# Where the second MoE's raw weight loads stand in the load queue of a fused attention, ELU MoE and SoLU MoE

## The chip, the cores and the metric

The kernel runs on one core of a Trainium2 chip. The metric is the device time in microseconds (us). The engines are TensorE (PE in the profile), VectorE (DVE), ScalarE (ACT), GpSimd (POOL) and SyncE (SP), which here issues all transfers.

## What is computed

The reference has three stages, one behind the other:

```python
# attention, keys and values averaged over groups of 8; 8 batches, 8 heads, 576 tokens, head size 64
scores = scale * q @ k_p.T;  attn = softmax(scores);  x = attn @ v_p      # x: 4608 tokens x 512
# first MoE, 512 -> 2048 -> 512
h = x @ w_in;  g = where(h > 0, h, exp(min(h, 0)) - 1);  x = g @ w_out
# second MoE, 512 -> 1024 -> 512
h = x @ w_in2;  solu = h * softmax(h);  ln = (solu - mean) / sqrt(var + 1e-6) * g_ln;  out = ln @ w_out2
```

The weights of both MoEs come as 64-bit floats. The kernel loads them as raw 64-bit integers and makes 32-bit floats of them by shifts and masks; then it splits every 32-bit operand of a large product into a high and a low part and computes three products (high x high, high x low, low x high).

## The kernel before, in words

The 4608 tokens are cut into nine blocks of 512 (j = 0 to 8). The first MoE goes block by block, each in 16 slots (f = 0 to 15), one per 128 columns of its hidden layer: `m_h1` (line 413) makes the hidden columns h by 12 matmuls and their exponential on ACT; `m_elu` (428) finishes them with two DVE instructions and makes the high part gh on ACT; `m_glo` (437) makes the low part gl on DVE; `m_o1` (444) multiplies them with the slot's rows of w_out by 12 more matmuls, one slot later. `w_out_split` (398) makes the two parts of these rows, on ACT and POOL. When a block is done, `m_out` (457) copies its result to SBUF and stores it to a DRAM buffer x1d (line 466, 1024 KB).

Attention runs beside this. There are 32 units (batch and pair of heads), each of four half steps (`att_half`, 269), spread over the slots so that block j+1 has its input before block j ends; the last unit is done in block 6. `att_load` (87) loads a unit's k, q and v two units ahead. k and v have one buffer each, q has two, so that a q load waits for the scores of two units before. At the start, a hand-ordered section (lines 633 to 642) does the first four units; then block 0 also converts all of the first MoE's weights (`conv_load` 312, `conv` 326, `conv_split` 348).

The second MoE's weights are prepared in sixteen pieces of 128 x 512, while the first MoE runs. `prep_load(c)` (362) loads piece c raw (512 KB, line 367) into a tile of the tag "cv", which has two buffers. `prep(c)` (371) takes a second tile of that tag and converts: an Abs on ACT (378), three DVE instructions (379 to 381), the high part on ACT (383 or 387) and the low part on DVE (384 or 388); it stores both parts (line 389, 512 KB) to a DRAM buffer w2d. In block 8 `fetch` (391) loads them back from there in eight loads (line 395, 1024 KB). The second MoE (`p2_load`, `p2_split`, `p2_h2`, `p2_T`, `p2_o`) follows block 8; `p2_load` (472) reads a block's x1d back (line 475, 1024 KB).

The order in which the program is written is not the order in which it runs. Outside the hand-ordered section a scheduler goes over the whole program before it is compiled. It keeps dependencies and buffers; on each engine, and on SyncE's queue, it issues what stands first in the program among the instructions that are ready by its own estimate of times. An instruction from much further down thus moves up when it is ready and its engine has nothing else. On the chip each engine then keeps that order.

Lines 686 to 689 are where the loads and conversions of the pieces stand in the program: in blocks 1 to 6, a load in the slots with f % 5 == 0 and a conversion in those with f % 5 == 2.

```python
if 1 <= j <= 6 and f % 5 == 0 and 3 * (j - 1) + f // 5 < 16:
    prep_load(3 * (j - 1) + f // 5)
if 1 <= j <= 6 and f % 5 == 2 and 3 * (j - 1) + f // 5 < 16:
    prep(3 * (j - 1) + f // 5)
```

f % 5 == 0 is true of f = 0, 5, 10 and 15; f % 5 == 2 of f = 2, 7 and 12.

Of the kernel before, what the change touches and what calls it, by code (L numbers as in the profile page):

```python
# [18 lines left out]
def kernel(  # L19
# [15 lines left out]
    nc = tc.nc  # L35
# [16 lines left out]
    x1d = dr.tile([P, KDM, NT], F32, name="x1d")  # L52
# [10 lines left out]
    def xtile(name, dt=F32R):  # L63
        return sb.tile([P, 4, 512], dt, name=name, tag="x", bufs=6)
# [4 lines left out]
    starts = [512 * j for j in range(NBLK)]  # L69
# [17 lines left out]
    def att_load(i, what="kqv"):  # L87
        b, p = units[i]
        if i < NP:
            if ("kq", p) not in st:  # L90
                kq = sb.tile([P, 4, 512], F32, name=f"kq{i}", tag="w", bufs=8).rearrange("p a f -> p (a f)")
                if p % 2 == 0:
                    st["v2"] = sb.tile([P, 4, 512], F32, name=f"v2{i}", tag="wo", bufs=4).rearrange("p a f -> p (a f)")
                n = P * POOL
                v_t = st["v2"][0:SK, (p % 2) * n:(p % 2 + 1) * n].rearrange("s (c t) -> s c t", t=POOL)
                st["kq", p] = (kq[:, 0:S], kq[:, S:2 * S], v_t)
            k_t, q_t, v_t = st["kq", p]
        else:
            k_t = sb.tile([P, S], F32, name=f"k{i}", tag="k", bufs=1)
            v_t = sb.tile([SK, P, POOL], F32, name=f"v{i}", tag="v", bufs=1)  # L100
            q_t = sb.tile([P, S], F32, name=f"q{i}", tag="q")
            st["ld", i] = (k_t, v_t)
        if "k" in what:
            nc.sync.dma_start(out=k_t, in_=kT[b, p])
        if "q" in what:
            nc.sync.dma_start(out=q_t, in_=qT[b, p])
            st["q", i] = q_t
        if "v" in what:
            nc.sync.dma_start(out=v_t, in_=v[b, p].rearrange("s h d t -> s (h d) t"))
# [141 lines left out]
    def att_late():  # L251
        t = st.pop("late")
        th, tl = (x[:, :, 0:2 * S - 1024] for x in xblk(2))
        nc.scalar.copy(th, t)
        nc.vector.tensor_tensor(tl, t, th.bitcast(F32), op=ALU.subtract)
# [13 lines left out]
    def att_half(n):  # L269

        while nload[0] < min(NU, n // 4 + 3):
            att_load(nload[0])
            nload[0] += 1
        i, r = divmod(n, 4)
        before = NP <= i - 1
        if r == 0:
            if i < NU:
                for _ in att_scores(i, single()):
                    pass
                att_max(i)  # L280
                att_exp(i)
        elif r == 1:
            if i < NU:
                att_soft(i)
            if before:
                att_T(i - 1, 1)
        elif r == 2:
            if before:
                att_V(i - 1, single())
                att_x(i - 1)  # L290
            if i + 1 < NU:
                att_setup(i + 1)
        elif r == 3:
            if i < NU:
                att_T(i, 0)
# [66 lines left out]
    def prep_load(c):  # L362

        g, kk = divmod(c, 4)
        raw = sb.tile([P, 512], I64, name="raw2", tag="cv", bufs=2)
        src = w_in2[kk * P:(kk + 1) * P, g * 512:(g + 1) * 512] if c < 8 else w_out2[(c - 8) * P:(c - 7) * P, :]
        nc.sync.dma_start(out=raw, in_=src)
        wraw["p", c] = raw
# [29 lines left out]
    def w_out_split(f):  # L398
        t = wo[f // 4]
        oh = sb.tile([P, 512], F32R, name="woh", tag="woh")  # L400
        ol = sb.tile([P, 512], F32R, name="wol", tag="wol")
        nc.scalar.copy(oh, t[:, f % 4, :])  # L402
        nc.gpsimd.tensor_tensor(ol, t[:, f % 4, :], oh.bitcast(F32), op=ALU.subtract)  # L403
        return oh, ol
# [2 lines left out]


    o1 = {}
    gt = {}  # L410
    wo_t = {}

    def m_h1(j, f):
        n = sizes[j]
        g, fo = f // 4, (f % 4) * P
        h = ps.tile([P, 512], F32, name="h1", tag="B")
        i = 0
        for kk in range(KDM):
            for a, x in ((wh, xh), (wl, xh), (wh, xl)):
                nc.tensor.matmul(  # L420
                    h[:, 0:n], a[g][:, kk, fo:fo + P], x[j][:, kk, 0:n], start=(i == 0), stop=(i == 3 * KDM - 1)
                )
                i += 1
        e = sb.tile([P, 512], F32, name="e", tag="e")
        nc.scalar.activation(e[:, 0:n], h[:, 0:n], AF.Exp)  # L425
        gt[j, f] = (e, h)

    def m_elu(j, f):
        n = sizes[j]
        e, h = gt[j, f]  # L430
        nc.vector.tensor_scalar(e[:, 0:n], e[:, 0:n], 1.0, 1.0, op0=ALU.min, op1=ALU.subtract)  # L431
        nc.vector.tensor_tensor(e[:, 0:n], e[:, 0:n], h[:, 0:n], op=ALU.max)  # L432
        gh = sb.tile([P, 512], F32R, name="gh", tag="gh")
        nc.scalar.copy(gh[:, 0:n], e[:, 0:n])  # L434
        gt[j, f] = (e, gh)

    def m_glo(j, f):
        n = sizes[j]
        e, gh = gt[j, f]
        g_l = sb.tile([P, 512], F32R, name="gl_", tag="gl")  # L440
        nc.vector.tensor_tensor(g_l[:, 0:n], e[:, 0:n], gh[:, 0:n].bitcast(F32), op=ALU.subtract)
        gt[j, f] = (gh, g_l)

    def m_o1(j, f):
        n = sizes[j]
        if f == 0:
            o1[j] = [ps.tile([P, 2, 512], F32, name=f"o1_{j}_{i}", tag="A") for i in range(2)]
        gh, g_l = gt.pop((j, f))
        oh, ol = wo_t.pop((j, f))
        for dm in range(KDM):  # L450
            acc = o1[j][dm // 2][:, dm % 2, 0:n]
            for m, (a, x) in enumerate(((oh, gh), (ol, gh), (oh, g_l))):
                nc.tensor.matmul(  # L453
                    acc, a[:, dm * P:(dm + 1) * P], x[:, 0:n], start=(f == 0 and m == 0), stop=(f == NF - 1 and m == 2)
                )

    def m_out(j):
        n = sizes[j]
        t = xtile(f"x1s{j}", F32)
        for dm in range(KDM):  # L460
            src = o1[j][dm // 2][:, dm % 2, 0:n]
            if dm % 2 == 0:
                nc.scalar.copy(t[:, dm, 0:n], src)
            else:
                nc.vector.tensor_copy(t[:, dm, 0:n], src)  # L465
        nc.sync.dma_start(out=x1d[:, :, starts[j]:starts[j] + n], in_=t[:, :, 0:n])


    NTILE = NT // P
# [183 lines left out]
    for si, (j, f) in enumerate(slots):  # L653
        if f == 0:
            credit = 0.0
            rate = max(need[j + 1] - step if j + 1 < NBLK else 0, 0) / (2.0 * NF)
        m_h1(j, f)
        for half in range(2):
            if half == 1:
                m_glo(j, f)  # L660
                if si:
                    pj, pf = slots[si - 1]
                    m_o1(pj, pf)
                    if pf == NF - 1:
                        m_out(pj)
                    if (j, f) == (1, 1):
                        att_late()
            credit += rate
            while credit > 0.999 and step < need[j + 1]:
                att_half(step)  # L670
                step += 1
                credit -= 1.0
            if half == 0:
                m_elu(j, f)
                if si == 0:
                    wo_t[j, f] = w_out_split(f)
            if j == 0 and (f % 2 == half or (f == 0 and half)):
                next_conv()
            if half == 1 and si + 1 < len(slots):
                nj, nf = slots[si + 1]  # L680
                wo_t[nj, nf] = w_out_split(nf)
        if j == 0 and f == NF - 1:
            while cq or sq_:
                next_conv()

        if 1 <= j <= 6 and f % 5 == 0 and 3 * (j - 1) + f // 5 < 16:
            prep_load(3 * (j - 1) + f // 5)
        if 1 <= j <= 6 and f % 5 == 2 and 3 * (j - 1) + f // 5 < 16:
            prep(3 * (j - 1) + f // 5)
        if j == NBLK - 1 and f % 4 == 3:  # L690
            fetch(f // 2 - 1)
            fetch(f // 2)
        if j == NBLK - 1 and f == 4:
            p2_load(0)
        if j == NBLK - 1 and f == 10:
            p2_load(1)
        if j == NBLK - 1 and f == 12:
            p2_split(0)
        if j + 1 < NBLK and f == NF - 1:
            while step < need[j + 1]:  # L700
                att_half(step)
                step += 1
    m_o1(NBLK - 1, NF - 1)
    m_out(NBLK - 1)


# [48 lines left out]
```

## Time and profile before

| | |
|---|---|
| median of 3 runs (lowest, highest) | 1414.27 us (1413.56, 1414.76) |
| the profiled execution's own time | 1413.46 us |
| its span | 1411.7 us |
| mean granted clock of TensorE, as a share of 2.4 GHz | 0.985 |
| busy: PE, DVE, ACT, POOL | 1362.0, 791.5, 588.8, 301.4 us |
| moved by transfers | 102.26 MB |
| raw loads of both MoEs | 53, of 512 KB |

The span goes from the first to the last instruction of one profiled execution; its own time is what the device reports for it, and the median is over other executions. All times in the rows below are from the start of the span. "Idle before" is the time for which an engine stood ahead of an instruction, with an arrow to the instruction or transfer that let it go on. The chain that ended last is followed back from the last instruction, at each step to what released it. SPq is SyncE's queue: its rows are the issue of a transfer, not its duration.

### The profile page before, as it was taken

Reading aid. Unit: us, or ns where it says so; the run is one execution under the profiler, and the core shown is the slowest. Engines: PE = TensorE matmul, PEld = TensorE weight load, DVE = VectorE, ACT = ScalarE, POOL = GpSimd, SP = SyncE. Lnnn points to the kernel's source line nnn. Section 1 sums busy time; section 2 is a strip of 40 time slices with the busy share of each in tenths; the row PEclk is TensorE's granted clock in tenths of the full one; section 3 lists DMA queues with packets and bytes.
Section 4 is the critical chain, followed back from the end, with each engine's and each line's share of the span. In section 5 each row is a group of like instructions: output and inputs, shape, how many; then the busy total and the mean of one; then the engine's idle time right before and its main releaser. Section 6 shows DMA issues by size and latency. Waiting matters only on the chain.

```text
span 1411.7 us, 16688 instructions
## 1 busy us (share of the span) xinstructions
PE 1362.0 (96%) x6368; PEld 1093.8 (77%) x6368; DVE 791.5 (56%) x1312; ACT 588.8 (42%) x1161; POOL 301.4 (21%) x245
## 2 busy tenths in 40 slices
PE   5788899999999999999999999999999999999998
PEld 3466677878878788788787788887888888888886
DVE  7799987886555555455554333433644554455442
ACT  3466554554444444344444333433433333333332
POOL 2345432322222322222223222221000000000000
PEclk7699999999999999999999999999999999999999
DMA  7355454461111011111010000314101110110000
GB/s 218 111 183 163 140 188 139 147 205 48 42 65 38 30 65 42 28 62 43 26 39 1 30 31 1 119 60 170 55 26 50 52 53 25 51 52 23 23 23 30
DMA packets 46991, 102.26 MB, mean 72 GB/s; under 512 B 4544, under 2 KB 12736, under 8 KB 45888
## 3 DMA queue, kind: packets, MB, share of 16 engines
q1 hardware_dynamic: 46912, 101.21, 21.5%
q8 instruction: 50, 0.82, 0.2%
q14 instruction: 29, 0.24, 0.1%
HBM read 73.93 MB, written 27.26 MB: 72 GB/s over the span
## 4 chain that ended last, share of the span: by engine, by line
PE 85%; DVE 8%; DMA 3%; ACT 2%; issue 1%; POOL 1%; SPq 0%; ACTq 0%; DVEq 0%
PE h L420 24%; PE o L453 24%; PE po L538 14%; PE h L494 14%; PE pt L523 2%; PE at L160 2%; PE at L235 2%; PE pt L211 2%; DMA raw<-in_w 1%; DMA q<-in_q 1%; DMA w2d<-cv 1%; DVE wo L343 1%; DVE wo L345 1%; DVE e L431 1%; DVE cv L345 1%
## 5 line engine op out<-in xcount | busy, mean ns | idle before, releaser
L403 POOL TENSOR_TENSOR wol<-wo,woh 128x512 fp32r<-128x512 f32 x144 | 206.6, 1435 | 541.0 <-ACT woh L402 541.0
L420 PE MATMUL h<-xh,wh 128*128 128x512 f32 x576 | 236.7, 411 | 0.8 <-ACT xh L248 0.4
L453 PE MATMUL o<-gh,woh 128*128 128x512 f32 x576 | 228.2, 396 | 6.6 <-ACT gh L434 3.4
L453 PE MATMUL o<-gh,wol 128*128 128x512 f32 x576 | 227.4, 395 | 0.8 <-POOL wol L403 0.8
L420 PE MATMUL h<-xl,wh 128*128 128x512 f32 x576 | 227.6, 395 | 0.0
L420 PE MATMUL h<-xh,wl 128*128 128x512 f32 x576 | 226.4, 393 | 0.7 <-POOL wl L360 0.7
L538 PE MATMUL po<-w,dhl 128*128 128x512 f32 x864 | 202.7, 390 | 1.8 <-ACT dhl L526 1.8
L431 DVE TENSOR_SCALAR e<-e 128x512 f32<-128x512 f32 x144 | 65.4, 454 | 242.1 <-ACT e L425 242.0
L538 PEld LDWEIGHTS po<-w,dhl 128*128 128x128 f32 x864 | 161.9, 188 | 36.5 <-ACT dhl L526 2.3
L494 PE MATMUL h<-w,x1h 128*128 128x512 f32 x576 | 186.5, 395 | 0.3 <-DVE x1s L465 0.3
L425 ACT ACTIVATE e<-h 128x512 f32<-128x512 f32 x144 | 85.9, 597 | 216.4 <-PE h L420 216.2
L434 ACT CAST gh<-e 128x512 fp32r<-128x512 f32 x144 | 89.5, 621 | 155.0 <-DVE e L432 155.0
L420 PEld LDWEIGHTS h<-xh,wh 128*128 128x128 f32 x576 | 108.9, 189 | 34.9 <-issue 13.6
L453 PEld LDWEIGHTS o<-gh,woh 128*128 128x128 f32 x576 | 108.8, 189 | 32.6 <-ACT gh L434 5.6
L453 PEld LDWEIGHTS o<-gh,wol 128*128 128x128 f32 x576 | 108.9, 189 | 24.9 <-POOL wol L403 1.3
L420 PEld LDWEIGHTS h<-xl,wh 128*128 128x128 f32 x576 | 108.7, 189 | 25.1 <-DVE xl L249 0.4
L420 PEld LDWEIGHTS h<-xh,wl 128*128 128x128 f32 x576 | 109.1, 189 | 22.0 <-POOL wl L360 1.4
L494 PEld LDWEIGHTS h<-w,x1h 128*128 128x128 f32 x576 | 108.2, 188 | 22.3 <-DVE x1s L465 0.7
L494 PE MATMUL h<-w,x1l 128*128 128x512 f32 x288 | 112.3, 390 | 0.0
L503 ACT ACTIVATE e<-h,sc 128x1024 f32<-128x1024 f32 x36 | 40.2, 1117 | 165.4 <-DVE sc L502 165.1
L513 POOL TENSOR_TENSOR sc<-sc,mhalf 128x1 f32<-128x1 f32 x36 | 19.7, 548 | 400.7 <-DVE sc L512 400.7
L402 ACT CAST woh<-wo 128x512 fp32r<-128x512 f32 x144 | 89.3, 621 | 35.4 <-PE o L453 31.0
(524 smaller groups left out, 1873.6 us busy)
## 6 DMA issues: line engine op xcount, KB each, us to landing
raw<-in_w SPq DMA_DIRECT2D x53, 512.0 KB
v<-in_v SPq DMA_DIRECT2D x32, 288.0 KB
x1d<-x1s SPq DMA_DIRECT2D x9, 1024.0 KB
x1r<-x1d SPq DMA_DIRECT2D x9, 1024.0 KB
out<-ot SPq DMA_DIRECT2D x36, 256.0 KB
w2d<-cv SPq DMA_DIRECT2D x16, 512.0 KB
w<-w2d SPq DMA_DIRECT2D x8, 1024.0 KB
k<-in_k SPq DMA_DIRECT2D x28, 288.0 KB
```

The lines of the kernel that those rows point to most:

```text
L160: nc.tensor.matmul(s[:, t * 2 * SK:(t + 1) * 2 * SK], q_t[:, o:o + P], kp, start=True, stop=True)
L211: nc.tensor.transpose(pt[0:SK, t * P:(t + 1) * P], es[:, 2 * t + h, :], ident)
L402: nc.scalar.copy(oh, t[:, f % 4, :])
L403: nc.gpsimd.tensor_tensor(ol, t[:, f % 4, :], oh.bitcast(F32), op=ALU.subtract)
L420: nc.tensor.matmul(h[:, 0:n], a[g][:, kk, fo:fo + P], x[j][:, kk, 0:n], start=(i == 0), stop=(i == 3 * KDM - 1))
L425: nc.scalar.activation(e[:, 0:n], h[:, 0:n], AF.Exp)
L431: nc.vector.tensor_scalar(e[:, 0:n], e[:, 0:n], 1.0, 1.0, op0=ALU.min, op1=ALU.subtract)
L434: nc.scalar.copy(gh[:, 0:n], e[:, 0:n])
L453: nc.tensor.matmul(acc, a[:, dm * P:(dm + 1) * P], x[:, 0:n], start=(f == 0 and m == 0), stop=(f == NF - 1 and m == 2))
L494: nc.tensor.matmul(h[:, g, :], a[c][:, kk, o:o + P], w[g][:, kk, :], start=(m == 0), stop=(m == 3 * KDM - 1))
L503: nc.scalar.activation(e, hv, AF.Exp, bias=sc[:, 0:1], accum_out=sc[:, 1:2])
L538: nc.tensor.matmul(po, a[:, c, :], w[c // 4][:, c % 4, :], start=(m == 0), stop=(m == 3 * NC2 - 1))
```

## The change

The condition for a load becomes f in (1, 6, 11), that for a conversion f in (3, 8, 13). A load is traced inside `tc.issue_after(...)`, which adds an edge without a semaphore: on SyncE's queue, the load must come behind the instruction named. For the first load of block j that is the store of block j-1's result (line 466), for the second and third the q load that was traced last (line 106). The instructions are kept in a dictionary `gate`.

```diff
         if "q" in what:
-            nc.sync.dma_start(out=q_t, in_=qT[b, p])
+            gate["ld"] = nc.sync.dma_start(out=q_t, in_=qT[b, p]).ins
             st["q", i] = q_t
...
     o1 = {}
+    gate = {}
...
-        nc.sync.dma_start(out=x1d[:, :, starts[j]:starts[j] + n], in_=t[:, :, 0:n])
+        gate[j] = nc.sync.dma_start(out=x1d[:, :, starts[j]:starts[j] + n], in_=t[:, :, 0:n]).ins
...
-        if 1 <= j <= 6 and f % 5 == 0 and 3 * (j - 1) + f // 5 < 16:
-            prep_load(3 * (j - 1) + f // 5)
-        if 1 <= j <= 6 and f % 5 == 2 and 3 * (j - 1) + f // 5 < 16:
+        if 1 <= j <= 6 and f in (1, 6, 11) and 3 * (j - 1) + f // 5 < 16:
+            with tc.issue_after(gate[j - 1] if f == 1 else gate["ld"]):
+                prep_load(3 * (j - 1) + f // 5)
+        if 1 <= j <= 6 and f in (3, 8, 13) and 3 * (j - 1) + f // 5 < 16:
             prep(3 * (j - 1) + f // 5)
```

## Rows read from the trace of the kernel before

**Rows 1.** The page, busy time, share of the span and instructions of each engine.

```profile
PE 1362.0 (96%) x6368; PEld 1093.8 (77%) x6368; DVE 791.5 (56%) x1312; ACT 588.8 (42%) x1161; POOL 301.4 (21%) x245
```

**Rows 2.** Windows: length; busy us (instructions) of PE, PEld, DVE, ACT, POOL; clock; DMA share; GB/s.

```profile
146.90:189.50 42.60, 39.15 (x184) 28.81 (x184) 39.63 (x57) 25.21 (x65) 15.46 (x10) 1.00 0.43 145
...
158.60:189.50 30.90, 29.13 (x138) 22.11 (x137) 28.04 (x42) 16.71 (x35) 9.06 (x6) 1.00 0.43 138
189.50:231.20 41.70, 38.53 (x185) 29.99 (x183) 32.22 (x53) 19.26 (x40) 12.55 (x9) 1.00 0.51 168
...
397.80:500.60 102.80, 102.80 (x497) 82.41 (x496) 55.99 (x94) 43.80 (x87) 27.85 (x20) 1.00 0.15 45
231.20:236.70 5.50, 5.50 (x20) 3.39 (x20) 3.64 (x5) 1.91 (x4) 1.08 (x1) 0.69 0.42 161
```

**Rows 3.** The chain that ended last, 215 to 360: start, us, what.

```profile
216.99 3.61 DMA raw<-in_w
220.62 3.96 DMA raw<-in_w
...
231.18 3.75 PE o L453 x10
...
248.05 1.23 PE at L160 x10
...
325.26 1.23 PE at L160 x10
...
350.97 1.23 PE at L160 x10
```

**Rows 4.** Timeline of ACT: start, us, engine, line, operation, idle before and releaser.

```profile
224.69 0.66 ACT L378 ACTIVATE cv<-raw 128x512 f32<-128x512 f32 x1 [3.75 <-DMA raw<-in_w]
...
258.30 0.68 ACT L378 ACTIVATE cv<-raw 128x512 f32<-128x512 f32 x1 [2.08 <-DMA raw<-in_w]
...
320.19 0.66 ACT L378 ACTIVATE cv<-raw 128x512 f32<-128x512 f32 x1 [3.07 <-DMA raw<-in_w]
...
989.90 1.15 ACT L482 CAST x1h<-x1r 128x512 fp32r<-128x512 f32 x2 [1.58 <-DMA x1r<-x1d]
```

**Rows 5.** Timeline of PE, 228 to 232.

```profile
229.36 0.50 PE L453 MATMUL o<-gh,woh 128*128 128x512 f32 x1 [0.57 <-ACT gh L434]
...
231.18 0.50 PE L453 MATMUL o<-gl__1748,woh 128*128 128x512 f32 x1 [1.09 <-DVE gl__1748 L441]
```

**Rows 6.** Tiles cv and raw: count, ns min/median/max, first and last start.

```profile
L378 ACT ACTIVATE cv<-raw x16: 658/669/682, 158.6 to 320.2; 128x512 f32<-128x512 f32 x16
...
L381 DVE SCALAR_TENSOR_TENSOR cv<-raw,cv x16: 629/686/1793, 164.9 to 322.6; 128x512 uint32<-128x512 uint32 x16
...
L345 DVE SCALAR_TENSOR_TENSOR wo<-raw,wo x8: 1212/1221/2306, 60.1 to 160.3; 128x1024 uint32<-128x1024 uint32 x8
```

**Rows 7.** Timeline of SyncE's queue: start and us of an issue, line, transfer.

```profile
189.49 0.63 SPq L466 DMA_DIRECT2D x1d<-x1s  x1
...
221.00 0.45 SPq L106 DMA_DIRECT2D q<-in_q  x1
...
314.44 0.33 SPq L367 DMA_DIRECT2D raw<-in_w  x1
...
706.13 0.53 SPq L466 DMA_DIRECT2D x1d<-x1s  x1
...
907.90 0.82 SPq L395 DMA_DIRECT2D w<-w2d  x2
...
981.86 0.52 SPq L466 DMA_DIRECT2D x1d<-x1s  x1
983.06 0.57 SPq L475 DMA_DIRECT2D x1r<-x1d  x1
```

**Rows 8.** Line 367, the pieces' raw loads; who waited for it (us, times).

```profile
L367 SPq DMA_DIRECT2D raw<-in_w x21: 327/328/1346, 146.9 to 314.4; - x21
...
  ACT cv L378: 11.9, 5
```

## The prediction

> **What bounds it now.** I went from the page to the table of windows, then to the chain that ended last, and from there into the timelines of the engines that the chain names. The page has TensorE (PE) busy for 96% of the span [rows 1]; that share hides one slow stretch, so the windows come next. In block 3 (397.80 to 500.60) PE has no idle time at all, with DVE busy 55.99 of 102.80 us and ACT 43.80 [rows 2]: a block there lasts as long as its matmuls. Earlier, PE stands: 30.90 - 29.13 = 1.77 us in 158.60 to 189.50 and 41.70 - 38.53 = 3.17 us in 189.50 to 231.20, with DVE at 28.04 and 32.22 us [rows 2]. In 231.20 to 236.70 PE is busy throughout, but at a granted clock of 0.69 on average: part of it ran at 1.2 GHz instead of 2.4, which costs 5.5 x (1 - 0.69) = 1.7 us [rows 2].
>
> The chain says what holds PE up. Its last pieces before PE takes over are a raw load, another raw load, and the way from there to PE at 231.18; behind that it is PE alone [rows 3]. The timeline of ACT shows it waiting 3.75 us for a raw load at 224.69, in the Abs of line 378 [rows 4], and that of PE shows it idle for 0.57 us at 229.36 for the gh that ACT makes next in its queue, and for 1.09 us at 231.18 for the gl that follows from gh [rows 5]. The last conversion of the first MoE's own weights starts at 160.3 [rows 6]; behind it only the second MoE's pieces set this stretch apart from block 3.
>
> Why are the pieces there at all? The code traces them into blocks 1 to 6, three to a block, but their Abs run from 158.6 to 320.2 [rows 6], in the tail of block 0, in block 1 and at the start of block 2 (the stores of the results of blocks 0 and 5 are at 189.49 and 706.13 [rows 7]). A raw load needs nothing but a free buffer, so the scheduler places it as early as one is free. Seven of the sixteen Abs lie from 158.6 to 224.7, the very stretch that loses time, and seven more from 258.30 to 320.19 [rows 4], where nothing is lost. A second thing is seen there: line 367 issued 21 loads for 16 pieces [rows 8], because the old condition holds at f = 15 too and loads the next block's first piece into a tile that nobody reads. ACT's waits for a raw load are 5, of 11.9 us in all [rows 8], as many as there are doubled loads, and the one of 224.69 belongs to such a piece: 216.99 is the load that nobody reads, 220.62 the real one, sent when the first had landed, 3.61 us later [rows 3].
>
> **The change, part by part.**
>
> (1) *The pieces leave the stretch.* A gate is only an order on SyncE's queue. The first load of block j now follows the store of block j-1's result; the first such store is at 189.49, the last at 706.13 [rows 7]. The second and third follow the newest q load traced by then. Counting half steps (step 35 when block 1 begins, one per slot) these are units 12 and 13; unit 12's goes out at 221.00 [rows 7], and the next one unit later, about 26 us (325.26 to 350.97 is one unit) [rows 3], since q has two buffers and waits for the scores of two units before. So the gates fall about where the code says, and block 0 has no piece left, block 1 three. What goes: the gaps, 1.77 + 3.17 us, and the 1.7 us of low clock, which followed on the last two of them: 6.6 us. Bounds: nothing (the gaps have another cause), or more, if slots that count as busy are slow too. By number of matmuls, 138 + 185 of them at block 3's 497 in 102.80 us take 66.8 of the 72.6 us, so 5.8 are lost, 7.5 with the clock; with the 3.45 - 1.77 = 1.68 us that PE stands from 146.90 to 158.60 [rows 2] the upper bound is 9.2. I take 6.6, where every term has a row.
>
> (2) *The pieces arrive in blocks 1 to 6.* Each issues a load, a store, four DVE instructions of at most 0.69 us (2.8) and two on ACT of some 0.67 (1.3) [rows 6]. Three a block bring DVE to 56.0 + 8.3 = 64.3 and ACT to 43.8 + 4.0 = 47.8 of 102.8 us; PE's matmuls hide them. What a piece costs under that cover is shown: from 248.05 to 325.26, three units of attention with seven pieces among them, 77.21 us pass, and three units without pieces are 3 x (350.97 - 325.26) = 77.13 [rows 3]: 0.08 us for seven. The other end is a piece of the bad stretch, 6.6 / 7 = 0.95 us. For the pieces that move I take 0.2 us together, by the row of the saturated stretch, since all of them go to stretches like it. If the cover is gone (ACT stands for a late load), the next thing late is gh, as at 229.36.
>
> (3) *The five doubled loads go*: 5 x 512 KB less to move, five instructions less on SyncE, and the delay of the real load. Nobody but their pieces waited for them, so the gain lies inside (1).
>
> (4) *What now queues behind what.* A raw load is an issue of about 0.33 us on SyncE [rows 7]. Its tile needs one of two cv buffers, and with the piece before it some 26 us away both are free, so the k load behind it is not held up. The gating store is not waited for, only issued first. The prep moves one slot together with its load. The fetches of line 395, which read what the pieces store, begin at 907.90, and the last piece now starts at about 706 [rows 7]: 200 us of cover, and no cost.
>
> One price has no row of its own: a 512 KB load right behind a 1024 KB store. The nearest are a 1024 KB load issued at 983.06 behind the store of 981.86 [rows 7], for which ACT stood until 989.90 [rows 4], so 6.84 us from issue to landing, and the bare 512 KB load, 3.61 us [rows 3]. I take 5.5, nearer the upper one, as it lies behind the same store; that is late by 2 us six times, and a stall of 3.07 us in a saturated stretch (the Abs of 320.19 [rows 4]) cost nothing, so it adds nothing to the sum. The Trainium skill, in DMA: Bandwidth & Descriptors, section Queues, rings and completion order, has a rule that speaks against the change here: on each DMA engine the descriptors are consumed in ring order, so that a load queued behind a store begins when the store's share is through. The 6.84 us agree with it. Taken alone, with each late landing handed on to PE, the rule gives the time of rival C.
>
> Sum, against the profiled execution: span 1411.7 - 6.6 + 0.2 = 1405.3; its own time is 1413.46, 1.76 above its span, so 1407.1. The median of the three runs, 1414.27, lies 0.81 above that execution: **1407.9**.
>
> **Rivals.**
>
> *B, the gaps outlive the pieces.* DVE is 91% busy in 158.60 to 189.50, for block 0 carries more attention than its share. If its 1.77 us stay, the fall of the clock comes all the same (1.7), and the three pieces left in block 1 cost 0.95 each (2.85), 6.3 of the 6.6 us are lost again: 1414.0. Against it: without three pieces DVE has 28.0 - 8.3 = 19.7 of 30.9 us to do, and the chain names the pieces.
>
> *C, the load lands late and ACT stands for it (slower).* Its place is the six loads gated by a store. An Abs can stand soon behind its load: at 314.44 one went out [rows 7], and ACT waited for it from 320.19 - 3.07 = 317.12 on [rows 4], 2.7 us later. With a landing after 6.84 us ACT stands 4.1 us, six times 24.8. What decides is the share of it that reaches PE: above 6.6 / 24.8 = 0.27 the change loses. At a half it is 12.4 - 6.6 = 5.8 us slower: 1420.1. For it: the 3.75 us at 224.69 cost PE 0.57 + 1.09 us, a share of 0.44. Against it: the 3.07 us cost nothing, and every such stall would lie in a saturated block.
>
> *D, the gates do not hold*: if the gating transfers were issued far ahead, the loads would bunch as before, 1414.3. But stores come once a block and q loads once a unit.
>
> *E, more comes back*, up to the bound in (1): 1414.3 - 9.2 + 0.2 = 1405.3.
>
> **How the numbers follow.** Forecast 0.72; its own range is 1406 to 1411, since the fall of the clock may stay (1.7 us) and thirteen pieces may cost 0.1 us each (1.3). E 0.08, B 0.11, D 0.02, C 0.07. The range of 1403.5 to 1413.0 takes in the forecast and E, with 1.8 us below E's bound for a shift of the scheduler's order that no row shows, and the milder half of B; C, D and the rest of B are left out, less than 2 in 10. A measurement of this kernel can tell about 0.2%, 2.8 us, from no change. Faster: the forecast and E, 0.80, less 0.01 for its upper end; no change: B and D, 0.13; slower: C with the 0.01, 0.08.
>
> **What would show it.** In the profile after, line 367 issues 16 loads, the first behind the first store of a result and the last past 700 us; the Abs of line 378 are spread over blocks 1 to 6; PE has next to no idle time from 158.6 to 231 and its clock stays at 1.00 there; the fetch of 907.90 comes 6 to 7 us earlier. The forecast is wrong if ACT waits several us for raw loads in blocks 1 to 6 with PE idle at line 453 behind them (C), or if PE's gaps ahead of 231 stay with no piece near them (B).

## The result, and the profile after

The kernel after took 1402.75 us (median of six runs, 1402.09 to 1405.73), the kernel before 1414.51 in the same comparison: a ratio of 0.9915, 95% interval 0.9898 to 0.9931. A second comparison of the same two kernels gave 1404.11 against 1413.55, ratio 0.9933, interval 0.9919 to 0.9946. The change is worth 9 to 12 us. The forecast was 1407.9 with a range from 1403.5: the direction and the mechanism came out, the size did not. The first comparison fell 0.75 us below the range; the second lies 0.6 us inside it.

Where the time went is seen best in the start times of PE's slots. The instructions of PE stand in the same order in both kernels, so a matmul can be set beside its twin. Two twins are the first output matmul of slot 11 in block 0 and that of slot 9 in block 2, thirty slots later. Timeline of PE, kernel before:

```profile
151.58 0.39 PE L453 MATMUL o<-gh,woh 128*128 128x512 f32 x1
...
354.80 0.39 PE L453 MATMUL o<-gh,woh 128*128 128x512 f32 x1
```

The same two in the kernel after:

```profile
149.52 0.39 PE L454 MATMUL o<-gh,woh 128*128 128x512 f32 x1
...
343.75 0.39 PE L454 MATMUL o<-gh,woh 128*128 128x512 f32 x1
```

The thirty slots took 203.22 us before and 194.23 after: 8.99 us less. From the second twin to the end of the span are 1411.7 - 354.80 = 1056.90 and 1400.4 - 343.75 = 1056.65 us, no difference that matters. The rest, 151.58 - 149.52 = 2.06 us, lies ahead of the first piece, where both kernels run the same instructions in the same order; the experiments show that it is no part of the change.

Windows of the kernel after, in the order of [rows 2]: length, busy us (instructions) of PE, PEld, DVE, ACT and POOL, clock, DMA share, GB/s.

```profile
158.60:189.50 30.90, 30.90 (x153) 25.01 (x152) 22.77 (x36) 14.65 (x30) 8.01 (x7) 1.00 0.32 99
182.00:284.20 102.20, 102.20 (x495) 81.95 (x494) 65.23 (x106) 46.35 (x92) 27.50 (x20) 1.00 0.23 76
...
397.80:500.60 102.80, 102.80 (x498) 82.41 (x496) 66.36 (x108) 46.69 (x93) 28.18 (x20) 1.00 0.23 76
```

In these windows PE has no idle time and the clock is at its upper level, 2.4 GHz; block 1 (182.00 to 284.20) is a saturated block like the others. The window of 397.80 to 500.60, with its three pieces, has DVE at 66.36 and ACT at 46.69 us, where it had 55.99 and 43.80 without [rows 2], and PE is as busy as it was.

SyncE's queue after the change, to be set beside [rows 7]: start and us of an issue.

```profile
181.63 0.62 SPq L467 DMA_DIRECT2D x1d<-x1s  x1
182.35 0.57 SPq L367 DMA_DIRECT2D raw<-in_w  x1
...
212.68 0.34 SPq L106 DMA_DIRECT2D q<-in_q  x1
213.07 0.42 SPq L367 DMA_DIRECT2D raw<-in_w  x1
...
695.08 0.53 SPq L467 DMA_DIRECT2D x1d<-x1s  x1
695.70 0.58 SPq L367 DMA_DIRECT2D raw<-in_w  x1
...
896.85 0.81 SPq L395 DMA_DIRECT2D w<-w2d  x2
```

The loads stand right behind their gates, the first at 182.35 and the last at 695.70; the fetch of w2d begins at 896.85 instead of 907.90 [rows 7]. What ACT does with them, by the view of line 378 (first and last start, then what ended its waits: us, times):

```profile
L378 ACT ACTIVATE cv<-raw x16: 661/668/676, 188.3 to 701.6; 128x512 f32<-128x512 f32 x16
...
  DMA raw<-in_w: 11.3, 16
```

All sixteen Abs now wait for their load, 0.7 us each on average, and none for a store; PE waits for nothing between 150 and 800, as far as its own list of waits shows. In the kernel before the same view had two kinds of wait:

```profile
  DMA raw<-in_w: 11.9, 5
  DMA w2d<-cv: 11.3, 7
```

The prediction spoke of the five waits for a load alone. As much time went to waits for a piece's store, which gives its cv buffer back.

### The profile page after: what moved, and what is told of

It is laid out like the page before. It is cut to its first block, busy times and chain, and to the rows that moved or that the text cites. A ratio compares the mean times of both kernels' runs of the same rounds, so it can differ in the third digit from the quotient of the medians.

```text
span 1400.4 us, 16659 instructions
## 1 busy us (share of the span) xinstructions
PE 1355.5 (97%) x6368; PEld 1093.1 (78%) x6368; DVE 799.4 (57%) x1312; ACT 588.7 (42%) x1161; POOL 299.1 (21%) x245
## 4 chain that ended last, share of the span: by engine, by line
PE 89%; DVE 6%; ACT 1%; DMA 1%; issue 1%; POOL 0%; SPq 0%; ACTq 0%
PE h L421 26%; PE o L454 26%; PE po L539 14%; PE h L495 14%; PE at L160 2%; PE pt L524 2%; PE at L235 2%; PE pt L211 2%; DVE wo L343 1%; DMA k<-in_k 1%; DVE wo L345 1%; DMA v<-in_v 1%; DVE wo L341 1%; DVE cv L345 0%; ACT es L180 0%
## 5 line engine op out<-in xcount | busy, mean ns | idle before, releaser
L403 POOL TENSOR_TENSOR wol<-wo,woh 128x512 fp32r<-128x512 f32 x144 | 201.7, 1401 | 534.0 <-ACT woh L402 534.0
L421 PEld LDWEIGHTS h<-xh,wh 128*128 128x128 f32 x576 | 108.6, 189 | 34.7 <-issue 13.6
```

Of the source, the lines that this page charges most:

```text
L421: nc.tensor.matmul(h[:, 0:n], a[g][:, kk, fo:fo + P], x[j][:, kk, 0:n], start=(i == 0), stop=(i == 3 * KDM - 1))
```

## The experiments

Every kernel below was measured by the same two twins, which leaves the start out (v_on_pool, which changes the start itself, stands at the end and not in the table). Each row is one profile. The table gives the start of the first twin, the time of the thirty slots, and what the first five, the next ten and the last fifteen of them took longer than in the kernel after (33.31, 64.31 and 96.61 us). The first five end with block 0, and the next ten lie in block 1.

```
kernel         first    thirty    first 5   next 10   last 15   all
after          149.52   194.23
again_after    151.14   194.22     -0.01      0.00      0.00    -0.01
before         151.58   203.22      2.93      5.92      0.14     8.99
again_before   151.11   204.80      2.95      7.62      0.00    10.57
no_double      149.13   203.90      2.87      3.24      3.56     9.67
gate_double    150.64   194.23      0.00      0.01     -0.01     0.00
gate_block0    152.26   196.74      0.03      0.00      2.48     2.51
three_early    150.53   196.96      2.64      0.08      0.01     2.73
no_dve         150.03   201.33      4.31      1.48      1.31     7.10
block0_es2     152.35   197.18      0.03      0.13      2.79     2.95
block0_cv3     154.23   194.61      0.00      0.14      0.24     0.38
nodouble_cv3   155.30   200.18      4.89      0.82      0.24     5.95
```

**Is the start part of it?** Both kernels once more, with no edit. Kernel again_before:

> The kernel before, unchanged, for a second profile. The instructions of the kernels before and after stand in the same order on every engine up to about 147 us, yet the profile after is 2.1 us ahead by 86 us already. Theory (start-up differs from run to run, the change has no part in it): this profile's slot starts up to 86 us differ from the first profile's by 1 to 2 us either way, and from 150 to 240 us it loses again about 9 us against a steady slot. Rival (the change sets the start too, through the code's layout or the queue): this profile repeats 62.1 and 86.2 us for the first and fourth slot's output matmuls within 0.3 us.

Kernel again_after:

> The kernel after, unchanged. Theory (8.9 us come from 150 to 240 us, the rest is start-up): ratio to the kernel before about 0.9935 (1405), with the first slots anywhere between 60.8 and 62.1 us. Rival (all 11.3 us belong to the change): ratio 0.9915 to 0.992 again, and 60.8 and 84.2 us for the first and fourth slot again.

Measured: 1414.56 us for the kernel before, one execution; for the kernel after the ratio of 0.9933. The twins of again_before and, behind them, of again_after, timeline of PE:

```profile
151.11 0.39 PE L453 MATMUL o<-gh,woh 128*128 128x512 f32 x1
...
355.91 0.39 PE L453 MATMUL o<-gh,woh 128*128 128x512 f32 x1
```

```profile
151.14 0.39 PE L454 MATMUL o<-gh,woh 128*128 128x512 f32 x1
...
345.36 0.39 PE L454 MATMUL o<-gh,woh 128*128 128x512 f32 x1
```

This time both kernels reach the first twin within 0.03 us of each other, so the 2.06 us of the first profile were chance: in the first nine rows of the table, kernels whose engines run the same instructions in the same order until the first piece, it lies anywhere from 149.13 to 152.26. The second profile of the kernel before did not settle it as expected: the output matmuls of its first and fourth slot start at 62.25 and 85.78 us, 0.2 us later and 0.5 earlier than in the first profile, where 1 to 2 us had been expected. It is the second profile of the kernel after that does, with 61.59 and 85.77 for 60.79 and 84.18. The stretch behind the start is another matter: 194.23 and 194.22 us after, 203.22 and 204.80 before. In both pairs it costs the kernel before 9 to 10.6 us, and this agrees with the 9.5 us of the second comparison.

**Are the doubled loads the cause?** They can be taken away alone, and the gates can be had with them.

In no_double, against the kernel before:

```diff
-        if 1 <= j <= 6 and f % 5 == 0 and 3 * (j - 1) + f // 5 < 16:
+        if 1 <= j <= 6 and f in (0, 5, 10) and 3 * (j - 1) + f // 5 < 16:
             prep_load(3 * (j - 1) + f // 5)
```

> The kernel before without the five doubled loads, with no gate: the pieces stay bunched from 147 us on. Theory (a piece costs because its instructions stand in the queues of ACT and DVE while DVE is still the limit; the doubled loads only make some of the waits longer): a third of the gain at most, 2 to 4 us faster than before, with the fall of the clock near 232 us gone or moved. Rival (the doubled loads are the cause: ACT's five waits for raw loads, 11.9 us): 8 us or more faster, as the kernel after. Second rival (nothing but where the pieces stand counts): within 1 us of before.

In gate_double, against the kernel after:

```diff
-        if 1 <= j <= 6 and f in (1, 6, 11) and 3 * (j - 1) + f // 5 < 16:
-            with tc.issue_after(gate[j - 1] if f == 1 else gate["ld"]):
+        if 1 <= j <= 6 and f % 5 == 0 and 3 * (j - 1) + f // 5 < 16:
+            with tc.issue_after(gate[j - 1] if f == 0 else gate["ld"]):
                 prep_load(3 * (j - 1) + f // 5)
-        if 1 <= j <= 6 and f in (3, 8, 13) and 3 * (j - 1) + f // 5 < 16:
+        if 1 <= j <= 6 and f % 5 == 2 and 3 * (j - 1) + f // 5 < 16:
             prep(3 * (j - 1) + f // 5)
```

> The gates of the change, but the old slots and with them the five doubled loads (21 loads again). Theory (in a saturated block neither a doubled load nor the wait for the real one costs anything): the time of the kernel after within 1 us. Rival (the doubled loads cost wherever they stand, about 1.7 us each as at 229 us): 5 to 8 us slower than the kernel after.

Measured: no_double has a ratio of 0.9996 to the kernel before (0.9987 to 1.0005), no gain; gate_double has 0.9928 (0.9915 to 0.9941), the kernel after to within the intervals, and the same 194.23 us of thirty slots. The doubled loads cost nothing by themselves; the gates are the whole gain. My theory had given the doubled loads 2 to 4 us, and that was a miss. What took their place is in the view of line 378 in no_double:

```profile
L378 ACT ACTIVATE cv<-raw x16: 659/669/692, 156.2 to 297.9; 128x512 f32<-128x512 f32 x16
...
  DMA w2d<-cv: 23.0, 10
```

The waits for a raw load are gone, but the pieces follow each other faster, the last Abs at 297.9 instead of 320.2 [rows 6], and ACT now waits 23.0 us for the stores that give the buffers back, where it waited 11.3. Without the doubled loads the last fifteen slots lose 3.56 us, where they lost 0.14. That the doubled loads had kept the later pieces apart is my reading: in these slots the pieces start 10.3 us apart on average in the kernel before, 8.8 in no_double.

**Where does a bunched piece cost?** Kernel gate_block0 lets all sixteen go after block 0, three_early lets only the first three go before its end.

In gate_block0, against the kernel after:

```diff
-            with tc.issue_after(gate[j - 1] if f == 1 else gate["ld"]):
+            with tc.issue_after(gate[0]):
                 prep_load(3 * (j - 1) + f // 5)
```

> All sixteen loads gated by one store, that of block 0's result, and none doubled: the pieces run bunched again, but only from about 182 us on, when the first MoE's weights are converted and PE is saturated. Theory (pieces cost where they are bunched: with two cv buffers ACT waits for each piece's store and holds gh back, saturated block or not; 9.7 us for sixteen in the kernel without doubled loads): 4 to 8 us slower than the kernel after (1408 to 1411), ACT's waits at line 378 name w2d, PE has gaps for gl or gh between 185 and 330 us. Rival (pieces cost only while DVE is the limit, before 240 us): within 1 us of the kernel after, PE without gaps.

In three_early, against the kernel after:

```diff
-            with tc.issue_after(gate[j - 1] if f == 1 else gate["ld"]):
-                prep_load(3 * (j - 1) + f // 5)
+            if j == 1:
+                prep_load(f // 5)
+            else:
+                with tc.issue_after(gate[j - 1] if f == 1 else gate["ld"]):
+                    prep_load(3 * (j - 1) + f // 5)
```

> The kernel after, with block 1's three loads set free (they go to 147 us and on), the other thirteen gated as they were. Theory (each piece that runs between 150 and 190 us costs about 1 us, 2.9 us for three by the slot starts of the kernel before): 2.5 to 3.5 us slower than the kernel after, all of it lost between 150 and 190 us. Rival (the three only use room that DVE has): within 1 us.

Measured: gate_block0 0.9956 (0.9943 to 0.9968) and three_early 0.9951 (0.9938 to 0.9964), so 3.3 and 2.5 us more than again_after by the ratios, 2.51 and 2.73 us by the slots. The intervals of the ratios overlap that of again_after at their ends, so the slots carry this reading. For three_early this is what the theory gave, and it lies in the first five slots (2.64). For gate_block0 the kind is right and the size was too big, and the place is telling: ten slots of block 1 with bunched pieces lose nothing, the fifteen behind them 2.48 us. What ended most of the waits of line 378 in gate_block0, and then the longest wait of PE from 185 to 330 (us in total, times, longest):

```profile
  DMA w2d<-cv: 16.2, 10
```

```profile
PE o L454 <- DVE gl__2182 L442: 0.8, 1, 0.8
```

So a saturated block is no cover of itself; it covers pieces that are far enough apart, and bunched ones as long as ACT waits little for their stores: 2.6 us in two waits in the ten slots, 13.6 us in eight in the fifteen.

**What in a piece holds PE up?** Kernel no_dve takes the pieces' work on DVE away and keeps the rest of them.

```diff
         nc.scalar.activation(w, hw.bitcast(F32), AF.Abs, scale=2.0**-112)
-        nc.vector.tensor_scalar(wu, wu, 3, None, op0=ALU.logical_shift_left)
-        nc.vector.scalar_tensor_tensor(wu, lw, 29, wu, op0=ALU.logical_shift_right, op1=ALU.bitwise_or)
...
-            nc.scalar.copy(h, w)
-            nc.vector.tensor_tensor(l, w, h.bitcast(F32), op=ALU.subtract)
...
+        nc.scalar.copy(h, w)
```

> The kernel before with the pieces where they were, doubled loads too, but the four DVE instructions of each piece left out and its second ACT instruction made a plain copy: loads, stores, buffers and ACT's two instructions stay, and the second MoE gets weights that are not converted. Theory (ACT standing in a piece's Abs for a buffer or a load is what holds gh back): at least half of the loss stays, 1 to 5 us faster than before, with gaps of PE for gh. Rival (the pieces' 17.5 us of DVE work are the cost): 8 us or more faster than before, as the kernel after.

Measured: ratio 0.9984 (0.9973 to 0.9995), 7.10 us lost in the thirty slots. Without any DVE work of the pieces two thirds to four fifths of the loss stay, and in the first five slots, the tail of block 0, more is lost than in the kernel before (4.31 against 2.93 us). ACT's waits from 150 to 300, largest of the pieces (us, times, longest):

```profile
ACT cv L377 <- DMA w2d<-cv: 20.4, 8, 3.8
...
ACT cv L377 <- DMA raw<-in_w: 12.2, 5, 3.1
```

ACT stands 32.6 us at the Abs, and what is behind it in its queue stands too. The pieces are also denser than before, so the two parts of the price can't be read off as a sum.

The last three ask whether a third cv buffer would do what the gates do. To make room for it the attention weights es get two buffers instead of three; block0_es2, the control, is gate_block0 with that edit alone:

```diff
-        st["a", i] = (sb.tile([P, NG, SK], F32, name=f"es{i}", tag="es", bufs=3), vt)
+        st["a", i] = (sb.tile([P, NG, SK], F32, name=f"es{i}", tag="es", bufs=2), vt)
```

Kernels block0_cv3 (against block0_es2) and nodouble_cv3 (against no_double with the edit above) have the third buffer at the three places of the tag:

```diff
-            w2 = sb.tile([P, 2, 512], F32, name="cv", tag="cv", bufs=2)
+            w2 = sb.tile([P, 2, 512], F32, name="cv", tag="cv", bufs=3)
...
-        raw = sb.tile([P, 512], I64, name="raw2", tag="cv", bufs=2)
+        raw = sb.tile([P, 512], I64, name="raw2", tag="cv", bufs=3)
...
-        t = sb.tile([P, 2, 512], F32R, name="cv2", tag="cv", bufs=2)
+        t = sb.tile([P, 2, 512], F32R, name="cv2", tag="cv", bufs=3)
```

> The kernel with all loads gated by block 0's store, with two buffers instead of three for the attention weights es, to make room in SBUF. It is the control for the next run. Both theories: the time of that kernel, 1407.5, within 1.5 us, and 97.6 + 99.1 us for the fifteen slots from about 151 us on and the fifteen after them (196.7 in all).

> As the control, with a third cv buffer. Theory (ACT's waits for a piece's store, 16.2 us in 10, are what bunched pieces cost in a saturated block): the waits that name w2d go down to under 5 us and the thirty slots take 194.2 to 195 us, 2 us less than in the control. Rival (the bunched pieces' work on ACT and DVE is the cost, whatever they wait for): 196.5 us or more, as the pieces run even denser.

> The kernel before without doubled loads and without gates, with a third cv buffer (and two es buffers). Theory (buffer waits are the cost): most of the 9.7 us that the thirty slots lose with two buffers go, 1404 to 1407. Rival (the pieces hold up DVE while it is the limit, buffers or not): half or more stays, 1408.5 to 1413, with the loss between 150 and 245 us.

Measured: medians of 1412.18, 1409.40 and 1415.23 us. The control missed its time by 4.7 us; the missing es buffer costs 2.1 of them behind the thirty slots (1408.3 - 349.53 = 1058.8 us from there to the end, against 1405.7 - 349.00 = 1056.7 in gate_block0), another 2.1 lie between the profiled execution, 1410.12 us, and the median, and no trace shows where. But its 197.18 us of thirty slots are near the 196.7 expected, and this is what the other two are held against. With the third buffer the thirty slots of block0_cv3 take 194.61, and the view of line 378 has one line of waits left, no store among them:

```profile
L378 ACT ACTIVATE cv<-raw x16: 652/665/677, 192.9 to 289.6; 128x512 f32<-128x512 f32 x16
...
  DMA raw<-in_w: 4.9, 8
```

This is the theory's case: in saturated blocks bunched pieces cost through the wait for the buffer, since with this wait 2.6 of the 2.95 us go, though the pieces run denser. How much of a wait reaches PE is another matter. View of line 378 over the last fifteen slots, kernel before (258 to 354.8) and, behind it, no_double (252.9 to 353):

```profile
  DMA raw<-in_w: 6.7, 3
  DMA w2d<-cv: 2.2, 3
```

```profile
  DMA w2d<-cv: 8.8, 4
```

ACT stands 8.9 us in the one and 8.8 in the other, yet the first loses 0.14 us and the second 3.56. So ACT's standing is no price by itself. Whether the kind of wait or the spacing of the pieces makes the difference is not shown.

In nodouble_cv3 the last fifteen slots behave the same way (3.56 to 0.24), but the first five lose 4.89 us, more than with two buffers. Nearly all of it is one wait of PE and the low clock behind it, 0.72 on average from 178 to 184, between the two levels of 1.2 and 2.4 GHz:

```profile
178.73 0.50 PE L453 MATMUL o<-gh,woh 128*128 128x512 f32 x1 [2.77 <-ACT gh L434]
```

For the rival speaks that DVE is busy for 27.71 of the 28 us from 150 to 178. Against it as the only cause: the Abs that stands right ahead of this gh in ACT's queue had waited 0.99 us for a raw load, and no_dve loses 4.31 us in the same five slots without any DVE work of the pieces. In the tail of block 0 a piece costs with or without waits for a buffer. The price is much the same everywhere: three pieces fall into these slots in the two profiles of the kernel before, in no_double and in three_early, five in no_dve and nodouble_cv3, and each costs 0.86 to 0.98 us. Which part of a piece costs it there stays open. The time of nodouble_cv3 lies above what either theory gave. With a third buffer the first twin also comes at 154 or 155 us, perhaps because the conversions of block 0 share the tag, which no run tests; so no part of this is a better kernel.

**Is there more to win at the start?** Before the first twin DVE is busy nearly all the time (86.14 of the 89.50 us from 60 us on in the kernel after). In v_on_pool, against the kernel after, the averages of v of units 4 to 9 go to GpSimd.

```diff
-            if early:
+            if i < 10:
                 pool_tree(vr, v_t)
```

> The kernel after, with the v averages of units 4 to 9 moved from DVE (1.2 us each) to GpSimd's tree of three additions. What is left to win lies before 160 us, where DVE is busy all the time (9.9 to 10 of 10 us) and PE is not. Theory (DVE is the limit there): 1 to 4 us faster than the kernel after. Rival (DVE and GpSimd slow each other down, 2.2 us instead of 1.2 for line 343 beside GpSimd): no gain, or slower.

Measured: ratio to the kernel before 1.0008 (0.9997 to 1.0019), 10 us slower than the kernel after: in time the rival, and more. The thirty slots take 194.75 us; the loss lies ahead of them, with the first twin at 161.02. In the view of the tile vr, who waited for it, v_on_pool and then the kernel after:

```profile
  PE at L235: 7.1, 3
```

```profile
  PE at L235: 5.5, 3
```

So the attention matmuls wait only 1.6 us longer for the averages, and the loss is not explained by that. Windows up to the last conversion of a weight of the first MoE, in the same order:

```profile
0.00:166.50 166.50, 118.62 (x513) 87.52 (x514) 137.27 (x171) 82.74 (x213) 78.50 (x72) 0.87 0.49 158
```

```profile
0.00:159.70 159.70, 120.58 (x534) 89.35 (x535) 136.92 (x179) 84.61 (x216) 67.31 (x55) 0.93 0.52 165
```

DVE has five averages of 6.04 us in all less to do and is busy as long as before (137.27 against 136.92 us), because others of its instructions take longer: the thirteen of line 432 take 14.60 us instead of 6.40. GpSimd is busy 11 us longer beside it. This fits the rival's mechanism, though not at the line that it named; that GpSimd is what slows DVE here is not shown. Nothing tried here beats the kernel after.

## Why the prediction was right in kind and too small

*(1) The pieces leave the stretch: right, and mis-sized. This is the step that failed.* I took 6.6 us for the gaps and the low clock; in the very profile from which I took it, the slots lost 8.99 us, and in the second 10.57. The error is in adding up PE's idle column. A matmul is listed with 0.39 to 0.40 us, but in a run of them the next one starts 0.23 us after it (231.52 to 231.75 below); the listed time runs on into the gap. The matmuls on both sides of the gap of 1.09 us that [rows 5] lists at 231.18, timeline of PE, kernel before:

```profile
229.69 0.40 PE L453 MATMUL o<-gh,wol 128*128 128x512 f32 x1
...
231.52 0.40 PE L453 MATMUL o<-gh,woh 128*128 128x512 f32 x1
231.75 0.39 PE L453 MATMUL o<-gh,wol 128*128 128x512 f32 x1
```

From 229.69 to 231.52 two starts should take 0.46 us; they take 1.83, so this gap costs 1.37 us where its row says 1.09. All seven gaps of 158 to 232 together can be had from the twins. The matmul of 231.52, behind the last gap, and that of 236.70, behind the low clock, in the kernel before:

```profile
236.70 0.40 PE L420 MATMUL h<-xh,wl 128*128 128x512 f32 x1
```

Their twins in the kernel after:

```profile
222.12 0.40 PE L454 MATMUL o<-gh,woh 128*128 128x512 f32 x1
...
225.72 0.40 PE L421 MATMUL h<-xh,wl 128*128 128x512 f32 x1
```

From the first twin to 231.52 are 79.94 us, in the kernel after 72.60: the seven gaps cost 7.34 us where their rows list 4.94. From there to 236.70 are 5.18 against 3.60 us: the low clock cost 1.58, where I took 1.7. Together that is 8.92 of the 8.99. I had the other count beside it: by number of matmuls 7.5 us, and 9.2 as the upper bound. The text took the sum of rows as the safer one. It was the lower one, by construction. The chance of 0.08 for rival E followed from that.

The 2.39 us between 6.6 and 8.99 are half of the miss. The forecast for the profiled execution was 1407.1 us, and the one after took 1402.24, 4.86 less; 2.06 of them are the start of these two profiles, which is chance. The range's lower end stood 1.8 us below E, and by the profiles the time fell below it only with both; the second comparison, at 1404.11, did not. Nor is the loss one number: 8.99 and 10.57 us in two profiles of one kernel.

*(2) What a piece costs in blocks 1 to 6: right for this change, and for a wrong reason.* 0.2 us were predicted; behind the second twin the kernel after is not slower, with eleven pieces in that stretch where there were none (1056.65 against 1056.90 us). The price of 0.95 us in the bad stretch was near enough too: three_early pays 2.73 us for three. But I laid the free pieces to the saturated block as such. no_double and gate_block0 show bunched pieces losing 2.5 to 3.6 us in saturated slots, and block0_cv3 shows that this goes with the wait for a buffer. The row that I used (0.08 us for seven pieces) was of pieces that waited 2.2 us for buffers in all.

*(3) The doubled loads: right.* No gain of their own: 0.9996 without them, and gate_double, which has them, runs like the kernel after.

*(4) The queue: right.* The loads stand behind their gates as reckoned, and PE waits for nothing between 150 and 800. The price without a row, a raw load behind a store, was put at 5.5 us between 3.6 and 6.8. The first of them, timeline of ACT:

```profile
188.28 0.67 ACT L378 ACTIVATE cv<-raw 128x512 f32<-128x512 f32 x1 [0.77 <-DMA raw<-in_w]
```

It was issued at 182.35 and landed by 188.28: 5.9 us. The other five behind a store were used 5.9 to 6.2 us after their issue, the ten behind a q load 3.7 to 4.6. The rule of the Trainium skill on ring order (DMA: Bandwidth & Descriptors, section Queues, rings and completion order) agrees with that lateness. That the order is the whole reason no run shows. What the rule did not decide is whether anybody feels it.

*The rivals.* B fell: no gap outlives the pieces. C's mechanism is there, ACT stands at each of the sixteen loads, for 11.3 us in all, but at most 1.6 us at a time and with a share of zero reaching PE. D fell by the queue's rows. E, with 9.2 us, was nearest to what the change is worth; its chance of 0.08 was too low for a bound that the count of matmuls supported.

*The start* was not in the prediction at all: profiles differ by up to 3 us before the first piece. 2.06 us of the first comparison of traces were that, and without the second pair of profiles they would have been put down to the change.

## What to carry to other kernels

A scheduler that hoists low-priority work as far as buffers allow can bunch it where it hurts; an order edge to something that paces the program (a store per block, a load per unit) spread it here at no cost that the traces show. The price of a stall on TensorE is read from the starts of twin matmuls, or from their count, not from the idle column. Before a stretch is called a cover, look at how far apart the work in it stood and what it waited for.

## What the runs showed of the hardware

In the second profile of the kernel before, the window that held the fall of the clock in the first [rows 2] has the same 0.69 on average, between the two levels of 1.2 and 2.4 GHz, again after gaps of PE.

```profile
231.20:236.70 5.50, 4.41 (x14) 3.08 (x14) 4.68 (x5) 2.26 (x5) 2.41 (x2) 0.69 0.56 190
```

The kernel after has no gap there and no fall. But the same gap can go either way. Near 102 us, where the kernels still run the same instructions, PE waits 2.18 us for gh in again_before and in again_after; the clock falls behind it in the first and not in the second, as their windows of 98 to 108 show, in this order:

```profile
98.00:108.00 10.00, 7.82 (x30) 5.83 (x29) 10.00 (x11) 4.96 (x9) 3.32 (x2) 0.83 0.40 134
```

```profile
98.00:108.00 10.00, 6.60 (x30) 4.87 (x29) 10.00 (x11) 5.08 (x9) 3.33 (x2) 1.00 0.42 134
```

The Trainium skill (TensorE: Matmul & The Clock Gate, section What's actually happening) calls the lower level the default, which activity lifts; that the falls shown here stand behind gaps of PE agrees with it. Which gap brings one these runs do not show.

PE can also lose time while it is listed as busy: 2.4 us over the seven gaps worked out above, over a quarter of the loss.
